# Experts of a fused attention and mixture kernel: columns reordered, conversion spread differently, gates loaded first, a branch hint moved

## The chip, the cores and the metric
The kernel runs on one core of a Trainium2 chip. The metric is the device time of one execution in microseconds; three runs of the kernel before gave a median of 917.99 us (917.13 to 922.21). The kernel after computes the same outputs.

## What is computed
The program has three parts, one behind the other.

```python
# attention, for every batch and head, token by token (B 4, H 8, S 768, D 48)
y[:, :, t] = einsum('bhd,bhde->bhe', q[:, :, t], state)
v_old = einsum('bhde,bhd->bhe', state, k_n[:, :, t])
state = state + beta_t * einsum('bhd,bhe->bhde', k_n[:, :, t], v_t - v_old)
# experts: 3072 tokens of 384 columns, 8 experts of width 1024
expert_idx = argmax((x_n @ e_n.T) / tau)          # one expert per token
out[mask] = gate_w[mask] * (relu(x[mask] @ w1[e]) @ w2[e])
# dense layers of width 2048
h = relu(x @ w_in);  result = (h * h) @ w_out
```

## The kernel before
**Order.** All instructions are put on the five engines in the order of the program text (a manual schedule), and each engine works through its own queue in order. TensorE multiplies; ScalarE and VectorE empty PSUM and convert; GpSimd issues indirect transfers; SP issues the plain transfers, all into one queue.

**Attention** runs in 24 steps of 32 tokens. `PW` (L385 on) ends a step: ScalarE copies the step's 128 x 384 outputs from a PSUM bank to the rows `XG` (L401), with the sign turned. From there the next step's `xrt` transposes them on TensorE for the router's logits (against the normalized expert embedding `enT` made in `router_consts`), `squares` takes the norm, and GpSimd scatters each row into its expert's slots of the DRAM buffer `xs` (L488). Beside the 384 columns a row carries 8 logits, a token number and a norm. The last rows of attention are placed for expert 0 by matmuls (`place`, `turn_x`), without the detour through `xs`; expert 0's first weights are loaded in three pieces during attention (`pre1`, L635 on).

**Splitting.** Every float32 product is done as three matmuls on an upper half and a lower half of each operand (`mm3`, L1172 to L1174). The upper half is written by ScalarE, the lower half by VectorE as the difference. For weights `weights(upto)` does this in pieces of 128 x 768: ScalarE's upper half at L620, and VectorE's lower half at L578 in the next `flush`. Per expert there are four pieces of second weights and four of the next expert's first weights.

**One expert** has capacity for 448 tokens. First half: eight blocks `fb` of 128 hidden columns, each nine matmuls into a PSUM bank (448 or 384 wide, by the count of tokens), then ScalarE's `hh` (L1273) and the 64-wide `ht` (L1274) and VectorE's lower half `hl` (L1275). Blocks 0 to 2 have banks of their own; blocks 3 to 7 and the short tile go round three banks. After each block `run(k)` hands out side work: weights, and steps of the conversion below. Second half: four token tiles in the order 0, 3, 1, 2 (tile 3 is the short one, 64 tokens), each with 24 matmuls (or the `tail` for the short one), an eviction `y` with the gate as scale (L1320), and an indirect scatter of `y` to `x2` by GpSimd (L1323); `run(9)` to `run(12)` follow them. In the second half `run` also pops `x_steps`: three times a VectorE transpose of the next expert's gathered columns `xe` (L1146), ScalarE's upper half (L1149) and VectorE's lower half (L1152). The transpose reads 32 columns at a stride of three elements, because the first weights of experts 1 to 7 lie in SBUF with three consecutive rows to a partition.

**Gates.** In expert 0 the softmax weights of all slots are worked out by the list `gops`, from columns of `xs` fetched by `load_gates` (L939 on; five transfers of 40-byte elements), behind `load_x(1)` in SP's queue.

**Conversion.** `q64` holds 132 steps: 22 pieces (numbers 2 to 23) of the dense layers' weights, six steps each (`w64`, L1084 on; the steps' VectorE lines are L1101, L1105, L1109, L1114, L1120 and L1117). A piece's first step reads its 512 KB load and issues that of the next piece (`fetch64(m + 1)`, L1082); the last writes to `wscr`. How many steps each `run(k)` does stands in the tuples `n`.

**Overflow.** Behind `run(10)` of expert 0, `overflow` holds a long part for experts with more than 448 tokens, under a branch (L989) that all engines evaluate and that skips it here. `mark_branch_hint_location("over", "LikelyTaken")` puts a hint for that branch into the engines' queues. Behind the branch SP loads the next expert's second weights (`load_w2`, four transfers, L1166).

Of the kernel before, what the change touches and what calls it, by code (L numbers as in the profile page):

```python
# [13 lines left out]
AF = mybir.ActivationFunctionType  # L14
ALU = mybir.AluOpType
# [7 lines left out]
def kernel(  # L23
# [16 lines left out]
    nc = tc.nc  # L40
    V, G, A, PE = nc.vector, nc.gpsimd, nc.scalar, nc.tensor
    NT, DM = out.shape
# [342 lines left out]
    def PW(s):  # L385
        g, i = divmod(s, 4)
        for hq in range(2):
            for b in range(4):
                PE.matmul(
                    YP[C * b : C * b + C, hq * 192 : hq * 192 + 192],  # L390
                    PL2[g][:, b, i, hq],
                    Wb[hq][:, b].rearrange("p f e -> p (f e)"),
                    start=s + hq == 0,
                    stop=True,
                    skip_group_check=True,
                )
        if i == 0:
            XG[g] = rp.tile([128, 4, ROW], F32, name="XG", bufs=3)
            G.tensor_copy(XG[g][:, :, XT].bitcast(I32), tok_i[:, 4 * g : 4 * g + 4])
            G.memset(XG[g][:, :, XT + 2 :], 0.0)  # L400
        A.activation(XG[g][:, i, 0:DM], YP[:, :DM], AF.Copy, scale=-1.0)  # L401
        if s >= NS - 2:
            hi, lo = [kept[0][:, (2 * i + j - 4) * DM : (2 * i + j - 3) * DM] for j in range(2)]
            A.activation(hi, XG[g][:, i, 0:DM], AF.Copy)
            lows.append(lambda: V.tensor_tensor(lo, XG[g][:, i, 0:DM], hi.bitcast(F32), ALU.subtract))
            oh = kept[0][:, 4 * DM + (i - 2) * CAP : 4 * DM + (i - 1) * CAP]
            more.append(([hi, lo], oh))
# [136 lines left out]
    def router_consts():  # L544
        nc.scalar.dma_start(itau, moe_tau.rearrange("(a b) -> a b", a=1).broadcast_to([128, 1]))
        emb = rp.tile([E, DM], F32, name="emb")
        nc.scalar.dma_start(emb, moe_expert_emb)
        jk = rp.tile([128, DM], F32, name="junk")[:E]
        es = rp.tile([E, 4], F32, name="es")
        A.activation(jk, emb, AF.Square, accum_out=es[:, 0:1])  # L550
        ops = []
        newton(ops, es[:, 1:2], es[:, 0:1], es[:, 2:3], magic[:E, :1])
        ops.append(lambda: V.reciprocal(itau, itau))
        ops.append(lambda: V.reciprocal(es[:, 1:2], es[:, 1:2]))
        ops.append(lambda: V.tensor_scalar(emb, emb, es[:, 1:2], None, ALU.mult))

        def turn():
            for kc in range(KD):
                PE.transpose(XP[:, kc * E : (kc + 1) * E], emb[:, kc * 128 : (kc + 1) * 128], ident[:E, :E])
            A.activation(enT.rearrange("p a e -> p (a e)"), XP[:, : KD * E], AF.Copy)  # L560

        ops.append(turn)
        return ops
# [71 lines left out]
    def pre1(a, fetch):  # L635

        if wbuf[0] is None:
            wbuf[0] = [None] * 4
        if fetch:
            raw1[a] = wp.tile([128, C, C], F32, name="AL", bufs=3).rearrange("p i j -> p (i j)")  # L640
            nc.sync.dma_start(raw1[a], moe_w1[0, a * 128 : a * 128 + 128])
            return
        wbuf[0][0] = wbuf[0][0] or cp.tile([128, 3072], F32R, name="W", bufs=5)
        V.tensor_copy(part(wbuf[0], 0, a * 1024, 1024), raw1[a])
# [340 lines left out]
    def overflow(mp):  # L985
# [3 lines left out]
        with tc.If(anyo > 0, label="over"):  # L989
# [18 lines left out]
            for e in range(E):  # L1008
                ne = nc.values_load(nover[0:1, e : e + 1], min_val=0, max_val=most)
                with tc.For_i(0, ne, 1) as i:  # L1010
                    b1 = mp.tile([128, 2304], F32, name="hb")
                    b2 = spare[0]
                    w, xg = b1[:, :1536], b1[:, 1536 : 1536 + ROW]
                    h, xt, y = b2[:, :1024], b2[:, 1024 : 1024 + DM], b2[:, 1024 + DM : 1024 + 2 * DM]
                    nc.sync.dma_start(xg, xs[bass.ds(i * 128 + (SLOTS + e * OVR), 128)])
                    ps = PT[0]
                    for kc in range(KD):
                        PE.transpose(ps[:, kc * 128 : kc * 128 + 128], xg[:, kc * 128 : kc * 128 + 128], ident)
                    A.activation(xt, ps[:, :DM], AF.Copy)
                    w1 = moe_w1[e].rearrange("(a p) f -> p a f", p=128)  # L1020
                    w2 = moe_w2[e].rearrange("(a p) f -> p a f", p=128)
                    for c in range(2):
                        nc.sync.dma_start(
                            w.rearrange("p (a f) -> p a f", a=KD), w1[:, :, c * 512 : c * 512 + 512]
                        )
                        ps = PT[1]
                        for fb in range(4):
                            for kc in range(KD):
                                o = kc * 512 + fb * 128
                                PE.matmul(  # L1030
                                    ps[:, fb * 128 : fb * 128 + 128],
                                    w[:, o : o + 128],
                                    xt[:, kc * 128 : kc * 128 + 128],
                                    start=kc == 0,
                                    stop=kc == KD - 1,
                                )
                        A.activation(h[:, c * 512 : c * 512 + 512], ps, AF.Relu)
                    ps = PT[2]
                    for c in range(2):
                        nc.sync.dma_start(w.rearrange("p (a f) -> p a f", a=4), w2[:, c * 4 : c * 4 + 4])  # L1040
                        for fb in range(4):
                            PE.matmul(
                                ps[:, :DM],
                                h[:, (c * 4 + fb) * 128 : (c * 4 + fb) * 128 + 128],
                                w[:, fb * DM : fb * DM + DM],
                                start=c + fb == 0,
                                stop=c + fb == 4,
                            )
                    ga, ops = gate(mp, xg[:, XL : XT + 2].unsqueeze(1), mp.tile([128, 4], F32, name="gsmo"), "gateo")
                    for o in ops:  # L1050
                        o()
                    A.activation(y, ps[:, :DM], AF.Copy, scale=ga)
                    G.indirect_dma_start(
                        out=x2,
                        out_offset=bass.IndirectOffsetOnAxis(ap=xg[:, XT : XT + 1].bitcast(U32), axis=0),
                        in_=y,
                        in_offset=None,
                        bounds_check=NT - 1,
                        oob_is_err=False,
                    )  # L1060
# [61 lines left out]
    def moe():  # L1122
# [14 lines left out]
        def x_steps(e):  # L1137
# [4 lines left out]
            for a in range(KD):  # L1142

                def turn(a=a):
                    x = xt[a] = mp.tile([128, CAP], F32, name="xt")
                    V.transpose(  # L1146
                        x.rearrange("p (u t) -> p u t", t=C), xe[e].rearrange("p u (k a) -> p a u k", a=KD)[:, a]
                    )
                    A.activation(xh[e][:, a], x, AF.Copy)  # L1149

# [64 lines left out]

        w_pieces()
        load_w2(0)
        load_x(1)
        t2k = mp.tile([128, 512], F32, name="t2k", bufs=3)
        gx = t2k[:, :320].rearrange("p (t e c) -> p t e c", t=4, e=E)  # L1220
        load_gates(gx)
        ga, gops = gate(mp, gx.rearrange("p t e c -> p (t e) c"), t2k[:, 320:448])
        ga = ga.rearrange("p (t e) -> p t e", t=4)
        rows_i = mp.tile([128, 4, E], I32, name="rows")
# [4 lines left out]
        for e in range(E):  # L1229
            wt = wbuf[e % 2]  # L1230
            def run(k, e=e):
# [4 lines left out]
                    weights(8 * e + (1, 1, 2, 3, 4, 4, 5, 5, 6, 8, 10, 11)[k - 1])  # L1236
                else:
                    weights(8 * e + (1, 1, 2, 3, 4, 4, 5, 5, 6, 7, 8, 8)[k - 1])
                n = (0, 0, 0, 0, 0, 0, 0, 0, 5, 5, 4, 0) if e == 0 else (0, 2, 0, 0, 0, 2, 0, 2, 4, 4, 3, 0)
                if last:  # L1240
                    n = (0, 2, 1, 0, 0, 2, 0, 2, 5, 4, 0, 0)
                for j in range(n[k - 1]):
                    if q64:
                        q64.popleft()()
# [10 lines left out]
            for fb in range(8):  # L1255
# [15 lines left out]
                        skip_runtime_bounds_check_because="it is only compared",  # L1271
                    )
                A.activation(hh[:, fb], ps[:, :384], AF.Relu)  # L1273
                A.activation(ht[:, fb], ps[:, 384:CAP], AF.Relu)  # L1274
                V.scalar_tensor_tensor(  # L1275
                    hl[:, fb], ps[:, :384], 0.0, hh[:, fb].bitcast(F32), ALU.max, ALU.subtract
                )
                run(fb + 1)
            if e == 0:
                while gops:  # L1280
                    gops.pop(0)()
# [10 lines left out]
            for i, t in enumerate((0, 3, 1, 2)):  # L1292
# [12 lines left out]
                def none(wt=wt, ps=ps, hh=hh):  # L1305
                    PE.matmul(ps[:, :64], hh[:, 7, :128], part(wt, 0, 3072, 64), start=True, stop=True)

                if t < 3:
                    for fb in range(8):
                        o = 3072 + fb * DM  # L1310
# [2 lines left out]
                            part(wt, 0, o, DM), part(wt, 1, o, DM), fb == 0, fb == 7,  # L1313
                        )
                else:
                    if e == 0:
                        tc.mark_branch_hint_location("over", "LikelyTaken", engines=ENGINES)
                    by_count(e, tail, none)
                y = mp.tile([128, DM], F32, name="y", bufs=2)
                A.activation(y[128 - n :], ps[128 - n :, :DM], AF.Copy, scale=ga[128 - n :, t, e : e + 1])  # L1320
# [151 lines left out]
```

## Time and profile before

| | us |
|---|---|
| median of 3 runs (lowest, highest) | 917.99 (917.13, 922.21) |
| the profiled execution | 918.82 |
| its span, first to last instruction | 917.0 |
| TensorE busy with matmuls | 851.9 |
| VectorE busy | 605.8 |
| ScalarE busy | 443.2 |
| GpSimd busy | 102.8 |

Attention takes the span up to about 268 us, the experts up to about 507, the dense layers the rest. Rows of a timeline give start and length in us, engine, line and operation; in brackets how long the engine was idle before, and what ended that. A row of the windows view gives a stretch and its length, then busy time and count of PE, PEld (the loads of weights), DVE, ACT and POOL, the granted clock, the share of the transfer engines and GB/s. ScalarE is named ACT, VectorE DVE, TensorE PE, GpSimd POOL, SP's queue SPq; a q behind an engine's name is its sequencer. Tile names are the program's: `wb` and `W` are weights' halves, `t4k` the conversion's input, `lb` a buffer whose parts hold second weights, `ht` and a conversion's intermediate.

### The profile page before, as it was taken

To read this page: it belongs to the slowest core of one execution; us is meant where nothing else is said; L and a number is where in the kernel's file an instruction comes from. 1 tells how busy PE (TensorE), PEld (TensorE's weight loads), DVE (VectorE), ACT (ScalarE), POOL (GpSimd) and SP (SyncE) were. 2 spreads that over 40 slices of the span, in tenths; PEclk is the share of its full clock that TensorE was granted. 3 is DMA by queue.
4 is the path that set the end of the run, shared out by engine and by line. 5 is a ranking of instruction groups with operands and counts; after the bars stand their busy time and mean duration, and the time that the engine had idled before them with its cause. 6 is when DMAs were issued, how large, how long until landed. Compare 5 with 4: busy or idle time off the path is not lost.

```text
span 917.0 us, 21827 instructions
## 1 busy us (share of the span) xinstructions
PE 851.9 (93%) x8775; PEld 777.3 (85%) x8775; DVE 605.8 (66%) x1499; ACT 443.2 (48%) x1074; POOL 102.8 (11%) x138
## 2 busy tenths in 40 slices
PE   4668989989987999999999999999999999999998
PEld 2446767667775989899888899999999999999998
DVE  6999899999777799889888762607061533425150
ACT  2246777778843565556555652515051423324140
POOL 3012103212210222122222100000000000000000
PEclk7587899999999999999999999999999999999999
DMA  8795775441139697788764632010010102020000
GB/s 331 243 281 178 227 222 145 166 153 62 67 115 198 217 299 217 216 251 237 236 216 159 182 87 44 1 39 15 18 35 18 35 9 44 9 44 1 26 1 27
DMA packets 110735, 116.27 MB, mean 127 GB/s; under 512 B 72771, under 2 KB 89258, under 8 KB 110624
## 3 DMA queue, kind: packets, MB, share of 16 engines
q1 hardware_dynamic: 102400, 88.39, 33.7%
q0 software_dynamic: 8064, 26.35, 7.8%
q8 instruction: 75, 1.23, 0.6%
q14 instruction: 36, 0.29, 0.1%
q10 hardware_dynamic: 160, 0.01, 0.0%
HBM read 82.61 MB, written 32.89 MB: 126 GB/s over the span
## 4 chain that ended last, share of the span: by engine, by line
PE 54%; DVE 5%; DMA 3%; issue 2%; ACT 2%; another core or an unknown queue 0%; POOL 0%; SPq 0%; DVEq 0%; POOLq 0%; ACTq 0%
PE gp L1172 7%; PE gp L1174 7%; PE gp L1173 7%; PE xp L1172 4%; PE xp L1174 4%; PE xp L1173 4%; PE sp L1173 3%; PE sp L1172 3%; PE sp L1174 3%; PE yp L1172 3%; PE yp L1174 3%; PE yp L1173 3%; DMA t4k<-in_moe_w_out_dram 1%; PE gp L1300 1%; DMA lb<-in_moe_w_dram 1%
## 5 line engine op out<-in xcount | busy, mean ns | idle before, releaser
L1380 DVE TENSOR_TENSOR t4k<-t2k 128x384 f32<-128x384 f32 x128 | 71.4, 558 | 199.7 <-ACT t2k L1379 197.7
L272 DVE TENSOR_TENSOR TL<-TL,tmp 128x135 f32<-128x135 f32 (+15 forms) x186 | 60.9, 338 | 1.8
L264 DVE TENSOR_TENSOR tmp<-AL,TL 128x135 f32<-128x135 f32 (+15 forms) x186 | 60.6, 337 | 1.6
L1172 PE MATMUL xp<-wb,hh 128*128 128x384 f32 x184 | 61.5, 334 | 0.0
L1173 PE MATMUL xp<-wb,hh 128*128 128x384 f32 x184 | 61.5, 334 | 0.0
L1174 PE MATMUL xp<-wb,hl 128*128 128x384 f32 x184 | 61.5, 334 | 0.0
L1323 POOL DMA_INDIRECT x<-y,rows x32 | 37.6, 1176 | 155.7 <-ACT y L1320 69.3
L1172 PE MATMUL sp<-xh,W 128*128 128x384 f32 (+1 forms) x156 | 52.6, 337 | 1.4 <-ACT xh L979 1.1
L1173 PE MATMUL sp<-xl,W 128*128 128x384 f32 (+1 forms) x156 | 52.5, 336 | 0.6 <-DVE xl L980 0.6
L1174 PE MATMUL sp<-xh,W 128*128 128x384 f32 (+1 forms) x156 | 52.4, 336 | 0.0
L1172 PE MATMUL gp<-wb,hh 128*128 128x384 f32 x152 | 51.2, 337 | 0.0
L1174 PE MATMUL gp<-wb,hl 128*128 128x384 f32 x152 | 50.8, 334 | 0.0
L1173 PE MATMUL gp<-wb,hh 128*128 128x384 f32 x152 | 50.8, 334 | 0.0
L367 ACT ACTIVATE Sb<-sp 48x384 f32<-48x384 f32 x92 | 44.7, 486 | 11.5 <-PE sp L357 10.5
L1173 PE MATMUL yp<-xl,W 128*128 128x384 f32 (+1 forms) x147 | 49.3, 335 | 0.0
L1172 PE MATMUL yp<-xh,W 128*128 128x384 f32 (+1 forms) x147 | 49.3, 335 | 0.0
L1174 PE MATMUL yp<-xh,W 128*128 128x384 f32 (+1 forms) x147 | 49.3, 335 | 0.0
L1404 ACT ACTIVATE y<-gp 128x384 f32<-128x384 f32 x12 | 5.9, 492 | 81.9 <-PE gp L1174 81.9
L1174 PE MATMUL gp<-xh,W 128*128 128x384 f32 (+1 forms) x135 | 45.2, 335 | 0.0
L1172 PE MATMUL gp<-xh,W 128*128 128x384 f32 (+1 forms) x135 | 45.2, 335 | 0.0
L1173 PE MATMUL gp<-xl,W 128*128 128x384 f32 (+1 forms) x135 | 45.2, 335 | 0.0
L1404 ACT ACTIVATE y<-xp 128x384 f32<-128x384 f32 x12 | 5.9, 492 | 80.2 <-PE xp L1174 80.2
(355 smaller groups left out, 2478.3 us busy)
## 6 DMA issues: line engine op xcount, KB each, us to landing
W<-in_moe_w_dram SPq DMA_DIRECT2D x28, 384.0 KB
hb<-in_moe_w_dram SPq DMA_DIRECT2D x24, 384.0 KB
W<-wscr SPq DMA_DIRECT2D x16, 384.0 KB
W<-in_kq_dram SPq DMA_DIRECT2D x11, 512.0 KB
wscr<-t2k POOLq DMA_DIRECT2D x22, 256.0 KB, 6.4
xs<-padrow POOLq DMA_DIRECT2D x8, 693.0 KB, 7.7
t4k<-in_moe_w_in_dram SPq DMA_DIRECT2D x10, 512.0 KB
xe<-xs SPq DMA_DIRECT2D x28, 168.0 KB
```

The lines of the kernel that those rows point to most:

```text
L264: V.tensor_tensor(tv[0], AL[:, j, j + 1 :].unsqueeze(1).broadcast_to([128, n, m]), T[:, :n, j : j + 1].broadcast_to([128, n, m]), ALU.mult,)
L272: V.tensor_tensor(T[:, : j + 1, j + 1 :], T[:, : j + 1, j + 1 :], tv[0], ALU.add)
L367: A.activation(Sb[hq][r : r + D, :, :, par, :], SP_[hq][r : r + D, 0:384].rearrange("p (b m e) -> p b m e", b=4, m=2), AF.Copy,)
L1172: PE.matmul(ps, hs, rh, start=first, stop=False)
L1173: PE.matmul(ps, hs, rl, start=False, stop=False)
L1174: PE.matmul(ps, ls, rh, start=False, stop=last)
L1300: PE.matmul(ps[64 * r : 64 * r + 64, :DM], ht[:, 4 * r + fb], w2raw[e][4 * r + fb], start=fb == 0, stop=fb == 3,)
L1323: to_x2 = lambda n=n, t=t, y=y, e=e: G.indirect_dma_start(out=x2, out_offset=bass.IndirectOffsetOnAxis(ap=rows_i[:n, t, e : e + 1].bitcast ...
L1380: V.tensor_tensor(s2, r, r, ALU.mult)
L1404: A.activation(y, ps[:, :DM], AF.Copy)
```

## The change
The rows' columns are written in the order in which the transposes of the experts read them, so that these read contiguous columns; the embedding, expert 0's first weights and the overflow part follow that order. The gates' columns are loaded ahead of expert 1's tokens. The conversion's 132 steps are spread 19, 6 x 16, 17 instead of 14, 6 x 17, 16. The 64-wide eviction goes behind `run`. The hint goes in front of expert 0's first token tile.

```diff
@@ PW
-        A.activation(XG[g][:, i, 0:DM], YP[:, :DM], AF.Copy, scale=-1.0)
+        A.activation(
+            XG[g][:, i, 0:DM].rearrange("p (q a k) -> p q k a", q=4, a=KD),
+            YP[:, :DM].rearrange("p (q k a) -> p q k a", q=4, a=KD),
+            AF.Copy,
+            scale=-1.0,
+        )
@@ router_consts (the transposes below it read jk instead of emb)
-        ops.append(lambda: V.tensor_scalar(emb, emb, es[:, 1:2], None, ALU.mult))
+        ops.append(
+            lambda: V.tensor_scalar(
+                jk.rearrange("e (q a k) -> e q k a", q=4, a=KD),
+                emb.rearrange("e (q k a) -> e q k a", q=4, a=KD),
+                es[:, 1:2], None, ALU.mult,
+            )
+        )
@@ pre1
-            nc.sync.dma_start(raw1[a], moe_w1[0, a * 128 : a * 128 + 128])
+            for m in range(4):
+                q, i = divmod(4 * a + m, KD)
+                rows = moe_w1[0, 96 * q : 96 * q + 96].rearrange("(k a) f -> a k f", a=KD)[i]
+                nc.sync.dma_start(raw1[a][32 * m : 32 * m + 32], rows)
...
@@ x_steps
-                        x.rearrange("p (u t) -> p u t", t=C), xe[e].rearrange("p u (k a) -> p a u k", a=KD)[:, a]
+                        x.rearrange("p (u t) -> p u t", t=C), xe[e].rearrange("p u (a k) -> p a u k", a=KD)[:, a]
@@ moe
         load_w2(0)
-        load_x(1)
         t2k = mp.tile([128, 512], F32, name="t2k", bufs=3)
         gx = t2k[:, :320].rearrange("p (t e c) -> p t e c", t=4, e=E)
         load_gates(gx)
+        load_x(1)
@@ run
-                n = (0, 0, 0, 0, 0, 0, 0, 0, 5, 5, 4, 0) if e == 0 else (0, 2, 0, 0, 0, 2, 0, 2, 4, 4, 3, 0)
+                n = (0, 0, 0, 0, 0, 0, 0, 0, 6, 5, 5, 3) if e == 0 else (0, 2, 0, 0, 0, 2, 0, 2, 4, 3, 3, 0)
                 if last:
-                    n = (0, 2, 1, 0, 0, 2, 0, 2, 5, 4, 0, 0)
+                    n = (0, 2, 1, 0, 0, 2, 0, 2, 5, 4, 1, 0)
@@ the first half's blocks
                 A.activation(hh[:, fb], ps[:, :384], AF.Relu)
-                A.activation(ht[:, fb], ps[:, 384:CAP], AF.Relu)
                 V.scalar_tensor_tensor(
                     hl[:, fb], ps[:, :384], 0.0, hh[:, fb].bitcast(F32), ALU.max, ALU.subtract
                 )
                 run(fb + 1)
+                A.activation(ht[:, fb], ps[:, 384:CAP], AF.Relu)
@@ the second half's tiles
+                if e == 0 and i == 0:
+                    tc.mark_branch_hint_location("over", "LikelyTaken", engines=ENGINES)
                 if t < 3:
...
                 else:
-                    if e == 0:
-                        tc.mark_branch_hint_location("over", "LikelyTaken", engines=ENGINES)
                     by_count(e, tail, none)
```

## Rows read from the trace of the kernel before

**Rows 1.** Windows view, a stretch of experts 0 and 1; busy us (and count) by engine.

```profile
320.00:340.00 20.00, 18.30 (x103) 17.41 (x102) 19.04 (x31) 11.25 (x24) 5.15 (x6) 1.00 1.01 298
```

**Rows 2.** Waits of PE, 290 to 600 us: total us, times, longest.

```profile
PE xp L1172 <- PEq L989: 5.2, 1, 5.2
PE ch L1174 <- DVE wb L578: 2.5, 2, 1.4
PE ch L1174 <- DVE W L578: 2.4, 2, 1.5
PE gp L1174 <- DVE hl L1275: 1.4, 1, 1.4
```

**Rows 3.** Windows view behind the branch, columns as in rows 1.

```profile
298.00:301.00 3.00, 2.85 (x9) 2.88 (x10) 1.72 (x3) 2.34 (x4) 0.29 (x1) 0.50 0.03 5
```

**Rows 4.** Timeline of PE, expert 1's last blocks, expert 2's first.

```profile
317.38 0.41 PE L1172 MATMUL sp<-xh,wb 128*128 128x384 f32 x1
...
319.05 0.33 PE L1172 MATMUL yp<-xh,wb 128*128 128x384 f32 x1
...
336.97 0.44 PE L1174 MATMUL ch<-xh,W 128*128 128x384 f32 x1 [1.49 <-DVE W L578]
```

**Rows 5.** Timeline of DVE in expert 0.

```profile
285.94 0.19 DVE L1225 COPY rows<-t2k 128x32 int32<-128x32 int32 x1 [3.60 <-DMA t2k<-xs]
...
292.39 0.36 DVE L1101 TENSOR_SCALAR W<-t4k 128x512 int32<-128x512 int32 x1
...
299.82 0.61 DVE L1322 SCALAR_TENSOR_TENSOR y<-gp,gate,y 64x384 f32<-64x384 f32 x1 [1.25 <-ACT y L1320]
...
302.20 0.69 DVE L1117 SCALAR_TENSOR_TENSOR t2k<-lb,t2k 128x512 f32<-128x512 f32 x1
```

**Rows 6.** Chain that ended last, in order of time: start, us, what.

```profile
310.82 8.23 DMA lb<-in_moe_w_dram
...
352.67 0.28 ACT y L1320
...
363.85 0.47 PE ch L1174
```

**Rows 7.** Groups by line and form, DVE transposes: count, busy us, mean ns.

```profile
L1146 DVE STREAM_TRANSPOSE xt<-xe 128x448 f32<-128x448 f32 x21 | 16.3, 775 | 0.0
L277 DVE STREAM_TRANSPOSE TTt<-TL 128x256 f32<-128x256 f32 x24 | 15.7, 672 | 0.0
...
L1201 DVE STREAM_TRANSPOSE y<-xe 128x384 f32<-128x384 f32 x21 | 12.0, 573 | 0.0
```

**Rows 8.** Timeline of ACT in an attention step, the eviction L401 and the work behind.

```profile
190.77 0.49 ACT L401 ACTIVATE XG<-yp 128x384 f32<-128x384 f32 x1
191.88 1.36 ACT L329 ACTIVATE Ub<-ch 32x192 f32<-32x192 f32 x4 [0.61 <-PE ch L308]
```

**Rows 9.** Timeline of SP's queue: x of expert 1, gates, expert 1's second weights.

```profile
272.58 2.80 SPq L1133 DMA_DIRECT2D xe<-xs  x4
275.43 7.09 SPq L943 DMA_DIRECT2D t2k<-xs  x3
282.56 1.34 SPq L945 DMA_DIRECT2D t2k<-xs  x2
...
309.36 1.42 SPq L1166 DMA_DIRECT2D hb<-in_moe_w_dram  x3
```

**Rows 10.** Timeline of DVE in expert 1's first half.

```profile
306.73 0.96 DVE L578 TENSOR_TENSOR wb<-W,wb 128x768 fp32r<-128x768 f32 x1 [1.05 <-DVEq L989]
...
323.58 0.55 DVE L1275 SCALAR_TENSOR_TENSOR hl<-yp,hh 128x384 fp32r<-128x384 f32 x1
...
324.91 0.42 DVE L1101 TENSOR_SCALAR W<-t4k 128x512 int32<-128x512 int32 x1
```

**Rows 11.** Timeline of POOL, the short tile's scatter in expert 0.

```profile
300.71 1.52 POOL L1323 DMA_INDIRECT x<-y,rows  x1 [5.85 <-DVE y L1322]
```

**Rows 12.** Timeline of DVE at the end of the last expert.

```profile
503.69 0.69 DVE L1117 SCALAR_TENSOR_TENSOR t2k<-lb,t2k 128x512 f32<-128x512 f32 x1
```

More of the change, by code (lines that the diff above doesn't have):

```diff
@@ L554, in router_consts @@
         ops.append(lambda: V.reciprocal(es[:, 1:2], es[:, 1:2]))
-        ops.append(lambda: V.tensor_scalar(emb, emb, es[:, 1:2], None, ALU.mult))
+        ops.append(
[5 more added lines that the diff above has]
+        )
         def turn():
             for kc in range(KD):
-                PE.transpose(XP[:, kc * E : (kc + 1) * E], emb[:, kc * 128 : (kc + 1) * 128], ident[:E, :E])
+                PE.transpose(XP[:, kc * E : (kc + 1) * E], jk[:, kc * 128 : (kc + 1) * 128], ident[:E, :E])
             A.activation(enT.rearrange("p a e -> p (a e)"), XP[:, : KD * E], AF.Copy)
@@ L1016, in overflow @@
                     ps = PT[0]
+                    A.activation(
+                        y.rearrange("p (q k a) -> p q k a", q=4, a=KD),
+                        xg[:, 0:DM].rearrange("p (q a k) -> p q k a", q=4, a=KD),
+                        AF.Copy,
+                    )
                     for kc in range(KD):
-                        PE.transpose(ps[:, kc * 128 : kc * 128 + 128], xg[:, kc * 128 : kc * 128 + 128], ident)
+                        PE.transpose(ps[:, kc * 128 : kc * 128 + 128], y[:, kc * 128 : kc * 128 + 128], ident)
                     A.activation(xt, ps[:, :DM], AF.Copy)
```

## The prediction, made before the change was run

> **What bounds the kernel now.** The windows view came first: in the experts' stage TensorE and VectorE are both close to full [rows 1], while the dense layers behind it keep TensorE busy throughout. So only idle time of TensorE between 268 and 515 us can be gained. The waits of TensorE name it [rows 2]: 5.2 us for its own sequencer at the branch around the overflow part (L989), 4.9 us in four waits for VectorE's lower halves of the next expert's first weights (L578), and 1.4 us for a lower half of the hidden tile. [...]
>
> The timelines and the chain then show who sets the pace. In expert 0 VectorE waits 3.60 us for the gates' columns and does gate arithmetic until 292.39 [rows 5]. The chain of waits runs through the load of expert 1's second weights [rows 6], not through TensorE's branch: what TensorE loses there, VectorE and the transfers lose as well.
>
> **The change part by part.** *Columns in VectorE's order.* 21 transposes of 128x448 read every third element in 0.775 us; 128x384 in order take 0.573 [rows 7], so 448 in order should take 0.573 x 448/384 = 0.67 at most, and less if part of it is fixed cost. I take 0.655: 0.12 saved each, 0.36 per expert. In return 24 evictions on ScalarE scatter their 384 elements 128 bytes apart. No row has such a write on ScalarE. Nearest is the 128x256 transpose that strides on both sides, 0.672 [rows 7], against 0.573 x 256/384 = 0.38 in order: 0.29 us for 256 elements, so between 0 and 0.43 for 384 if all of it is the write's. ScalarE idles 0.61 us behind this eviction in a step [rows 8], which covers that; after the last steps it is bare. I take 0.1 once, bounds 0 and 0.6. [...] The nine extra loads of weights lie steps ahead of their use, behind nothing that waits on SP; the reordered embedding is 8 rows, once. Both nothing; should the loads come late, the cast at L644 would wait for them.
>
> *Gates first.* Today x's four issues take SP 2.80 us from 272.58, then the gates' five 7.09 + 1.34, ending at 283.90 [rows 9]; they land 2.0 us later, at 285.94 [rows 5]. Issued first they end at 281.0 and land at 283.1. VectorE is free for them at 285.94 - 3.60 = 282.3. I take 282.7: all that follows on it is 3.2 us earlier, and TensorE's waits for the hidden tile go. x lands some 3 us later, still ahead of its first transpose.
>
> *The hint* moves from in front of the short tile to in front of the first tile, 24 matmuls (4 us) earlier on TensorE. [...]
>
> *Spread 19.* In expert 0's second half VectorE does the sixth step of a piece (0.69) and one more subtraction of about that size in the 1.25 us that it idles before 299.82 [rows 5]; with three faster transposes the short tile's y comes at 299.82 - 3.2 - 0.36 = 296.3. GpSimd scatters it [rows 11], and SP loads expert 1's second weights 309.36 - 300.71 = 8.65 us after that scatter's start [rows 9, 11], because the skipped branch waits for its landing: now at 305.8. VectorE goes on from 296.9: two lower halves (1.8), five steps (0.42 to 0.69, 0.58 in the mean: 2.9), the branch (1.05 [rows 10]), a lower half 0.9: 303.5. TensorE's first block of expert 1 ends there, some 6 us earlier than today.
> Then come five steps, a lower half, and steps 17 to 19, at about 308.6. Steps are six to a piece, so step 19 begins piece 5, and reads a 512 KB load that SP issues behind the four loads of expert 1's second weights. Today VectorE comes to it at 324.91 [rows 10] and sees no wait. The last of the four lands 8.23 us after its issue at 310.82 [rows 6], 9.7 after the first; the piece behind it lands 9.7 to 11.0 after (512 KB at 400 GB/s take 1.3). I take 10.2, so 316.0: **a new wait of 7.4 us on VectorE.** Queued behind it are the hidden tile's halves of expert 1, and with them PSUM banks. TensorE has banks for six blocks, done at 303.5 + 5 x 1.6 = 311.5; the seventh waits for the fourth half. VectorE gets there through the step 0.4, two halves 1.0, a weights' half 0.87, two steps 1.15 and two halves 1.0: 320.4, where the block begins at 317.38 now [rows 4]. TensorE is 3.0 late, and after some 9 us idle I expect the low clock again, 1.5 for about nine matmuls as after the 5.2 us [rows 3].
> On VectorE the eighth half, which ends at 324.1 now [rows 10], ends 10.1 after the wait, at 326.1. By VectorE, expert 2's first block resumes 336.97 - 324.1 = 12.9 later [rows 4, 10] less 0.9 (one step, three transposes): 338.1. By TensorE its first output tile comes 4.5 late, about 329.3; from there to the resumption expert 2 shows 363.85 - 352.67 = 11.2 [rows 6], less 0.8: 339.7. I take 339.4 against 336.97: **+2.4**, bounds +1.1 and +2.8.
>
> *16 each.* At the boundaries into experts 3, 5 and 6 VectorE has one step less (0.42 to 0.69) and two faster transposes ahead of the late half: 0.8 each, 2.4 in all, less what ScalarE's own order of evictions keeps. I take **-1.7**, bounds -2.4 and -0.5.
>
> *17 in the last expert.* One step is pushed behind the others, in front of the iota on GpSimd that the final gather waits for; VectorE's last step, 0.69, ends at 504.4 now [rows 12]. **+0.6**, bounds 0 and +0.7.
>
> *64-wide evictions later.* 0.1 us less before each upper half, and a bank that is freed behind a split. TensorE waits for VectorE there, so nothing; where a split waits for its load, the bank waits with it, at most 0.8 once.
>
> Sum: 2.4 - 1.7 + 0.6 + 0.1 = +1.4. The profiled execution took 918.82 (its span 917.0 and 1.8 around it), 0.83 above the median of 917.99. Profiled: 920.2; median: **919.4**.
>
> **The rivals.** *The load is no wait* (faster). If piece 5 lands by 308.6, expert 1 keeps its lead: -3.6 by the earlier weights' load and -0.9 by VectorE's lighter half, so -4.5 - 1.7 + 0.6 + 0.1 = -5.5: 912.5. Against it: it stands behind 1.5 MB in one queue. For it: the whole queue moves forward, and each microsecond of earlier landing is one gained.
> *The weights' load does not move* (slower). If it stays at 309.36, since the skipped branch waits for some other transfer, piece 5 lands at 319.6 and the seventh block comes 3.6 later than in my sum: +5.0, 923.0. It decides from a landing at about 319.2 on. Against it: the row before the load is GpSimd's scatter, which VectorE's y leads.
> *The scattered write.* If an eviction grows by more than the 0.61, each step pays the rest: 0.2 over would be 23 x 0.2 = 4.6, and 924.0 in all. The bound of 0.43 speaks against.
> *The hint does nothing.* TensorE then stands 5.2 us at the branch and comes to expert 1 near 304, still ahead of the wait on step 19: 919.4 too. [...]
>
> **How the numbers follow.** Forecast 0.55 (the hint working 0.35 or not 0.20), no wait 0.25, load unmoved 0.14, scattered write 0.06. A measurement of this kernel can tell about 0.5% (4.6 us) from no change: faster 0.25, same 0.55, slower 0.20. The range reaches from 911.5, below the first rival, to 924.0, over the second; outside lie about 0.10 of the first, and 0.10 of the second and third. The likeliest case alone: 917 to 922.
>
> **What would show it.** Right: the gates' first instruction on VectorE near 282.7; expert 1's first block near 299 to 304; a wait of several microseconds on VectorE before the conversion's first step (L1101) near 309 to 316, and TensorE's longest wait of the stage behind it; transposes near 0.65; about 0.6 less wait at each of three later boundaries. Wrong: no such wait (then faster), an eviction of the columns above 1.1 us, or the weights' load still at 309.

## The result, and the profile after

| | before | after |
|---|---|---|
| median of 8 runs, us | 920.34 | 929.39 |
| ratio, 95% interval | | 1.0090 (1.0063 to 1.0118) |
| profiled execution, its span, us | 918.82, 917.0 | 931.17, 929.4 |
| start of the experts' stage on TensorE | 267.83 | 270.55 |
| length of the experts' stage | 245.08 | 253.27 |
| from there to the end | 404.1 | 405.6 |

The kernel became slower by 0.9%, some 8 us. The stage is counted from the last matmul of the count of tokens (`xp<-cum,ones`) to the first product of the dense layers. Its length is given beside the ratios because attention's end varied from 267.6 to 274.1 us between the profiles below, with either order of the columns. Each length comes from one profiled execution; how much it varies between executions of one kernel was not measured. Of the 12.4 us between the two spans 2.7 lie in attention, 8.2 in the experts, 1.5 in the dense layers.

TensorE's waits of the kernel after, 290 to 620 us (line; total us, times, longest), against [rows 2]:

```profile
PE sp L1191 <- ACT lb L1297: 9.3, 2, 8.2
PE ch L1193 <- DVE wb L589: 3.9, 3, 2.2
PE ch L1193 <- DVE W L589: 1.7, 2, 1.0
PE sp L1191 <- ACT xh L993: 1.6, 1, 1.6
PE xp L1191 <- PEq L1003: 1.0, 1, 1.0
```

The stall at the branch fell from 5.2 to 1.0 and the wait for the hidden tile's half is gone. In their place stands one wait of 8.2 us, and it is for ScalarE's 64-wide eviction `ht` (L1297, tile name `lb`), not for VectorE. The timelines of expert 1 show how it comes about; first VectorE, SP's queue and TensorE:

```profile
311.24 0.69 DVE L1136 SCALAR_TENSOR_TENSOR t2k<-lb,t2k 128x512 f32<-128x512 f32 x1
318.88 0.43 DVE L1120 TENSOR_SCALAR W<-t4k 128x512 int32<-128x512 int32 x1 [6.94 <-DMA t4k<-in_moe_w_in_dram]
319.22 0.55 DVE L1293 SCALAR_TENSOR_TENSOR hl<-ch,hh 128x384 fp32r<-128x384 f32 x1
320.44 0.56 DVE L1293 SCALAR_TENSOR_TENSOR hl<-ch,hh 128x384 fp32r<-128x384 f32 x1 [0.67 <-ACT hh L1292]
...
324.06 0.56 DVE L1293 SCALAR_TENSOR_TENSOR hl<-sp,hh 128x384 fp32r<-128x384 f32 x1 [0.67 <-ACT hh L1292]
```

```profile
307.57 1.42 SPq L1185 DMA_DIRECT2D hb<-in_moe_w_dram  x3
309.03 0.50 SPq L1185 DMA_DIRECT2D lb<-in_moe_w_dram  x1
309.57 1.43 SPq L1101 DMA_DIRECT2D t4k<-in_moe_w_in_dram  x2
```

```profile
324.93 0.69 PE L1191 MATMUL sp<-xh,wb 128*128 128x384 f32 x1 [8.18 <-ACT lb L1297]
```

Step 19's first instruction waits 6.94 us for the load that SP issued behind the four of expert 1's second weights. It lands 318.88 - 307.57 = 11.3 us after the first of them. ScalarE in the same stretch:

```profile
308.49 0.46 ACT L1292 ACTIVATE hh<-ch 128x384 fp32r<-128x384 f32 x1
310.98 0.85 ACT L631 ACTIVATE wb<-hb 128x768 fp32r<-128x768 f32 x1 [2.03 <-DMA hb<-in_moe_w_dram]
319.81 0.22 ACT L1297 ACTIVATE lb<-ch 128x64 f32<-128x64 f32 x1 [7.98 <-DVE hl L1293]
319.93 0.48 ACT L1292 ACTIVATE hh<-ch 128x384 fp32r<-128x384 f32 x1
...
324.66 0.23 ACT L1297 ACTIVATE lb<-sp 128x64 f32<-128x64 f32 x1
```

ScalarE's 64-wide eviction of block 0 stood 7.98 us, until VectorE had its lower half of the same block, and with it every upper half behind it in ScalarE's queue. Both only read the bank, but one comes behind the other. Before, VectorE's half came behind ScalarE's two evictions; the waits of VectorE before, and of ScalarE after (285 or 290 to 520 us):

```profile
DVE hl L1275 <- ACT lb L1274: 13.2, 16, 2.6
```

```profile
ACT lb L1297 <- DVE hl L1293: 30.2, 32, 8.0
```

In the list of ScalarE's waits before no such line stands. So one read depends on the other: `ACT lb` waits for `DVE hl` 32 times after, 30.2 us in all, and never before. The direction turned with the order of the program's text, as these two lists show. Why the two reads of one bank are kept apart no run here shows.

### The profile page after: what moved, and what is told of

Read it like the earlier page. It is cut to its first block, busy times and chain, and to the rows that moved or that the text cites. A ratio compares the mean times of both kernels' runs of the same rounds, so it can differ in the third digit from the quotient of the medians.

```text
span 929.4 us, 21763 instructions
## 1 busy us (share of the span) xinstructions
PE 859.9 (93%) x8775; PEld 783.0 (84%) x8775; DVE 605.0 (65%) x1499; ACT 455.2 (49%) x1074; POOL 99.5 (11%) x138
## 4 chain that ended last, share of the span: by engine, by line
PE 54%; DVE 5%; issue 3%; DMA 3%; ACT 2%; POOL 0%; SPq 0%; POOLq 0%; ACTq 0%; DVEq 0%
PE gp L1191 7%; PE gp L1193 7%; PE gp L1192 7%; PE xp L1191 4%; PE xp L1193 4%; PE xp L1192 4%; PE sp L1191 3%; PE sp L1192 3%; PE sp L1193 3%; PE yp L1191 3%; PE yp L1193 3%; PE yp L1192 3%; DMA x<-y,rows 1%; DVE W L589 1%; DMA t4k<-in_moe_w_in_dram 1%
## 5 line engine op out<-in xcount | busy, mean ns | idle before, releaser
L357 PE MATMUL sp<-Wb,kL 128*48 128x96 f32 x736 | 46.3, 276 | 2.3 <-issue 1.7
L1191 PE MATMUL gp<-xh,W 128*128 128x384 f32 (+1 forms) x135 | 45.2, 335 | 0.0
```

Of the source, the lines that this page charges most:

```text
L357: PE.matmul(SP_[hq][64 * par : 64 * par + D, b * 96 : b * 96 + 96], kL2[g][:, i, b * 2 + hq], Wb[hq].rearrange("p b (m r) e -> p b r m e", ...
L1191: PE.matmul(ps, hs, rh, start=first, stop=False)
```

## The experiments

In each table row below "vs before" is the ratio with its interval, and in us the change that this ratio makes of the median of before measured beside it; "stage" is the length of the experts' stage in the profile (before 245.1, after 253.3).

**One part back.** Into the changed kernel: `u_ht` the 64-wide eviction in its old place, `u_spread` the old tuples of `n`, `u_ht_spread` both, `u_cols` the columns in the old order in all places.

```diff
@@ u_ht
                 A.activation(hh[:, fb], ps[:, :384], AF.Relu)
+                A.activation(ht[:, fb], ps[:, 384:CAP], AF.Relu)
...
                 run(fb + 1)
-                A.activation(ht[:, fb], ps[:, 384:CAP], AF.Relu)
@@ u_spread
-                n = (0, 0, 0, 0, 0, 0, 0, 0, 6, 5, 5, 3) if e == 0 else (0, 2, 0, 0, 0, 2, 0, 2, 4, 3, 3, 0)
+                n = (0, 0, 0, 0, 0, 0, 0, 0, 5, 5, 4, 0) if e == 0 else (0, 2, 0, 0, 0, 2, 0, 2, 4, 4, 3, 0)
...
-                    n = (0, 2, 1, 0, 0, 2, 0, 2, 5, 4, 1, 0)
+                    n = (0, 2, 1, 0, 0, 2, 0, 2, 5, 4, 0, 0)
```

`u_ht`:

> The changed kernel with its 64-wide eviction back in front of VectorE's half. Theory A (the eviction behind the split ties ScalarE to VectorE, as both read one PSUM bank and are kept apart there, so after the 6.9 us wait the upper halves come one by one): the seventh block of expert 1 begins about 4.4 us after that wait's end instead of 6.05, and the whole is 1.6 to 3.5 us faster than the changed kernel, +5.5 to +7.5 us against the kernel before. Rival B (only the wait on step 19's load counts): within 0.5 us of the changed kernel, +9. Rival C (attention's scattered write made the 9 us): +9 too.

`u_spread`:

> The changed kernel with the conversion spread as before (14, 6 x 17, 16). Theory A and B (step 19 waits for the 512 KB load behind expert 1's second weights): the 6.9 us wait on VectorE is gone and the 8.2 us wait of TensorE with it; 5 to 9 us faster than the changed kernel, 0 to +4 us against the kernel before. Rival C (attention): +7 or more remain, and TensorE's first block of expert 0 still starts some 2.7 us later than before.

`u_ht_spread`:

> Both of the two parts back. Theory A: the eviction also costs at the later boundaries, so -4 to +1 us against the kernel before, 1 to 3 us less than with the spread alone back. Rival B: the same as with the spread alone back, within 0.7 us. Rival C: +3 or more remain.

`u_cols`:

> The changed kernel with the columns in the old order in all places. Theory A and B: the write's extra 0.41 us per step is hidden in attention and the faster transposes give back about 0.1 us each where VectorE is late: between 1 us faster and 2 us slower than the changed kernel, +8 to +11 us against the kernel before. Rival C (the scattered write costs attention 2.7 us or more): 2.5 to 9 us faster than the changed kernel, 0 to +6.5.

| | vs before | us | stage |
|---|---|---|---|
| u_ht | 1.0016 (0.9991 to 1.0041) | +1.5 | 248.2 |
| u_spread | 0.9985 (0.9955 to 1.0014) | -1.4 | 246.3 |
| u_ht_spread | 0.9949 (0.9914 to 0.9983) | -4.7 | 241.5 |
| u_cols | 1.0109 (1.0076 to 1.0141) | +10.1 | 253.3 |

Attention (C) falls: with the columns back the loss stays, and with either of the other two back most of it goes. The spread's return brought some 10 us by the ratios, a little more than A said, and 7.0 us of the stage. B falls as well: the eviction alone is worth 0.74% of the 0.9% by the ratios, more than the 1.6 to 3.5 us that A gave it, and 5.1 us of the stage. Both back give -4.7, just under A's range, and a stage 4.8 us shorter than the spread alone back, where A had 1 to 3. `u_cols` lies in its range, and its stage is as long as that of after: beside the other parts the faster transposes gained nothing there.

The mechanism shows in VectorE's and TensorE's timelines of `u_ht`:

```profile
317.56 0.43 DVE L1120 TENSOR_SCALAR W<-t4k 128x512 int32<-128x512 int32 x1 [5.75 <-DMA t4k<-in_moe_w_in_dram]
317.91 1.01 DVE L1294 SCALAR_TENSOR_TENSOR hl<-ch,hh 128x384 fp32r<-128x384 f32 x2
...
320.76 1.01 DVE L1294 SCALAR_TENSOR_TENSOR hl<-sp,hh 128x384 fp32r<-128x384 f32 x2
```

```profile
321.93 0.66 PE L1191 MATMUL sp<-xh,wb 128*128 128x384 f32 x1 [3.58 <-DVE hl L1294]
```

ScalarE has worked ahead, so lower halves follow each other in pairs ("x2") without the 0.67 us gaps of the kernel after, and the seventh block starts 321.93 - 317.56 = 4.37 us behind the wait's end, where it was 324.93 - 318.88 = 6.05. The rest of the eviction's price lies later: counted from the stage's start, after stands 1.1 us behind `u_ht` where expert 2 begins, 1.8 at expert 4, 3.2 at expert 6, 5.3 at expert 7. In expert 6 the low clock adds to it (windows view from that expert's first block on, of after, then of `u_ht`; columns as in [rows 1]):

```profile
452.90:462.90 10.00, 8.82 (x34) 7.10 (x33) 8.01 (x14) 5.66 (x12) 2.79 (x4) 0.83 0.68 236
```

```profile
449.00:459.00 10.00, 9.07 (x44) 7.94 (x44) 6.99 (x12) 6.17 (x15) 3.17 (x3) 1.00 0.60 199
```

The first ten microseconds hold 34 matmuls at a granted clock of 0.83 and 44 at 1.00. Whether that clock is owed to the eviction is open (last section).

**Direction or place; the load; the hint.** `u_ht_mid` takes the eviction from behind the split, but leaves it behind VectorE's half in the text: ScalarE's order is that of `u_ht`. `u_load` issues step 19's load ahead of expert 1's second weights; `u_ht_load` is that with the eviction in its old place; `u_hint` has the hint in its old place.

```diff
@@ u_ht_mid
-                run(fb + 1)
                 A.activation(ht[:, fb], ps[:, 384:CAP], AF.Relu)
+                run(fb + 1)
@@ u_load, u_ht_load
-        if m < len(pieces64):
+        if m < len(pieces64) and m not in raw64:
...
                 if e == 0 and i == 1:
+                    fetch64(5)
                     overflow(mp)
```

`u_ht_mid`:

> The changed kernel with the 64-wide eviction ahead of the split again, but still behind VectorE's half in the program: ScalarE's order is the old one, and only who waits for whom differs (ScalarE's 64-wide read for VectorE's read of the same bank). Theory A (the tie to VectorE costs): most of the loss stays, +6.5 to +10 us against the kernel before, and in expert 1 ScalarE's 64-wide evictions still stand idle until VectorE's halves. Rival D (it is the place behind a split, whose load is late, that costs): like the kernel with the eviction fully back, +0 to +3.

`u_load`:

> The changed kernel with step 19's 512 KB load issued at the end of the second token tile of expert 0, ahead of expert 1's second weights in SP's queue. Theory A (that load's place in the queue makes the wait): VectorE's 6.9 us wait shrinks below 1 us, TensorE's 8.2 us wait to some 2 us, and the whole to between -3 and +2 us against the kernel before (the spread alone back gave -1.4). Rival E (the transfer engines are full then, wherever the load stands): a wait of 3 us or more stays and the whole is above +4.

`u_ht_load`:

> The same early load, and the 64-wide eviction back in front. Theory A: both losses gone with all gains kept, so below the kernel with spread and eviction back (-4.7): -8 to -4 us against the kernel before. Rival E: above -2.

`u_hint`:

> The changed kernel with the hint back in front of the short tile. Theory A (the hint starts the fetch, but expert 1 waits for its weights' halves anyway): TensorE stands some 5 us at the branch again, and the whole is within 2 us of the changed kernel, +7 to +11. Rival F (the stall shrank for another reason, such as the eviction's order): the stall stays near 1 us.

| | vs before | us | stage |
|---|---|---|---|
| u_ht_mid | 1.0214 (1.0179 to 1.0250) | +19.7 | 266.7 |
| u_load | 1.0006 (0.9981 to 1.0031) | +0.6 | 246.9 |
| u_ht_load | 0.9959 (0.9932 to 0.9985) | -3.8 | 242.0 |
| u_hint | 1.0080 (1.0052 to 1.0107) | +7.4 | 253.1 |

`u_ht_mid` settles the eviction, and beyond what A expected: with the same order on ScalarE, the direction of the dependency alone is worth 18.6 us of the stage (266.7 against 248.2). ScalarE's wait for VectorE doubles against after; in its queue the weights' splits now stand behind the eviction too:

```profile
ACT lb L1296 <- DVE hl L1293: 61.1, 59, 8.2
```

Behind the split, where the change put it, the eviction costs less than it does directly behind VectorE's half (stage 253.3 against 266.7). D falls.

In `u_load` VectorE comes to step 19 without a wait, as A expected:

```profile
312.15 0.69 DVE L1136 SCALAR_TENSOR_TENSOR t2k<-lb,t2k 128x512 f32<-128x512 f32 x1
312.75 0.42 DVE L1120 TENSOR_SCALAR W<-t4k 128x512 int32<-128x512 int32 x1
```

TensorE's wait for the eviction shrinks from 8.2 to 2.5 us. VectorE still waits 3.6 us for a load of the conversion in `u_load`, but in expert 0, in front of the first step. So step 19's wait was the place in the queue, and E falls. `u_ht_load`, at -3.8, misses the range of -8 to -4 by a little: without the wait the new spread is worth no more than the old one (stage 242.0 against 241.5).

`u_hint` has the stall of 4.9 us back and the changed kernel's time. The hint's new place is not all that decides: in nine profiles with it the stall was 1.0 to 1.8 in four and 4.5 to 5.4 in five, `u_ht` (5.2) among them, `u_ht_load` with the same place of the eviction among the short ones (1.5). So it is not the eviction's order (F). What it is stays open; that the hint starts a fetch, as A had it, was the author's guess, which no run shows. Between `u_hint` and the changed kernel the stall made no difference to the time.

**One part alone**, in the kernel before: `b_ht` the eviction, `b_spread` the tuples, `b_cols` the columns, `b_hint_gates` the gates' load and the hint. The diffs are the parts of the change itself.

`b_ht`:

> The kernel before with the 64-wide eviction moved behind VectorE's half and the split, and nothing else. Theory A (the tie of ScalarE to VectorE costs by itself): +3 to +6 us against the kernel before, most of it in experts 0 and 1. Rival G (it costs only beside the wait of step 19, which makes the tie felt): within 1.5 us of the kernel before.

`b_spread`:

> The kernel before with the conversion spread 19, 6 x 16, 17 and nothing else. Theory A (step 19's load lands behind expert 1's second weights, whatever stands ahead): a wait of 3 to 7 us on VectorE before that step's first instruction, +3 to +8 us. Rival H (without the gates' earlier load VectorE comes later than the load lands): no such wait, -2 to +1.

`b_cols`:

> The kernel before with the columns in the new order and nothing else. By the prediction's terms: transposes 0.65, the write 0.41 us longer but hidden: -2 to +1 us. Rival C (the write costs attention): +3 or more.

`b_hint_gates`:

> The kernel before with the gates' columns loaded first and the hint moved, and nothing else. By the prediction's terms: the gates' first instruction on VectorE some 3 us earlier after expert 0's start, TensorE's waits for the hidden tile gone, expert 1's second weights earlier by 2 to 4 us: -1 to -4 us. Rival (VectorE's gain is lost in its next wait): within 1 us.

| | vs before | us | stage |
|---|---|---|---|
| b_ht | 1.0048 (1.0013 to 1.0083) | +4.4 | 249.8 |
| b_spread | 1.0041 (1.0012 to 1.0071) | +3.8 | 251.5 |
| b_cols | 0.9950 (0.9922 to 0.9979) | -4.6 | 242.8 |
| b_hint_gates | 0.9976 (0.9951 to 1.0002) | -2.2 | 245.0 |

A holds for the eviction and the spread, G and H fall. Where the eviction costs was missed: only 1.8 of its 4.7 us lie ahead of expert 2, where A had most of it. `b_spread` shows the wait with the gates loaded late:

```profile
313.93 0.69 DVE L1117 SCALAR_TENSOR_TENSOR t2k<-lb,t2k 128x512 f32<-128x512 f32 x1
320.92 0.43 DVE L1101 TENSOR_SCALAR W<-t4k 128x512 int32<-128x512 int32 x1 [6.29 <-DMA t4k<-in_moe_w_in_dram]
```

In `b_hint_gates` the gates start 3.8 us earlier and expert 1's second weights are loaded 2.5 us earlier, as expected, but where expert 3 begins nothing of it is left (92.96 us after the stage's start, before 93.03). The stage is as long as before, and the ratio's interval reaches over 1, so the rival (the gain is lost in the next wait) is not excluded.

By stage lengths the parts add up: +4.7 +6.4 -2.3 -0.1 = +8.7, where the change as a whole has +8.2. The ratios' sum, +1.4, does not reach the whole's +8.3. The gap of 6.9 us is near what the five intervals (2.4 to 3.2 us to either side) leave together, 6.0 as the root of the sum of their squares, so whether the parts interact stays open. The columns alone gained more than expected. The fastest mixtures tried are `u_ht_spread`, columns, gates and hint without the spread and the eviction, and `b_cols`, the columns alone: both are below both kernels, and the ratios do not tell them apart.

## Why the prediction was wrong

Forecast 919.4 with a range to 924.0, measured 929.39. Of these 10.0 us, 2.35 lie in the base: the median of before was 917.99 in the three runs behind the forecast and 920.34 in the eight of the result. Moved by that, the range would end at 926.4, still below. Times on the trace below are counted from the stage's start, to take out attention's 2.7 us.

**The step that failed** is the last of the parts: "64-wide evictions later ... TensorE waits for VectorE there, so nothing; where a split waits for its load, the bank waits with it, at most 0.8 once." It asked only when the bank comes free. Who has to wait for whom to read it was not asked, although the edit turned that round: an engine that ran ahead was put behind the slower one, once per block, for 64 blocks of the stage, and at half of them it waited. Measured: 5.1 us of the stage in the changed kernel and 4.7 alone; between `u_spread` and `u_ht_spread` it is 4.8 and between `u_load` and `u_ht_load` 4.9, so four pairs of profiles agree.

**The term that was too small** is that of the spread with the lead ahead of it, +2.4. Much of its course came as forecast: the gates' first instruction 18.11 → 14.36 (predicted -3.2, measured -3.75), the second weights' load 41.53 → 37.02 (-3.6, -4.5), the wait from 41.4 to 48.3, 6.9 long (predicted 40.8 to 48.2, 7.4), and with the eviction back the seventh block 49.55 → 52.11, +2.6 (+3.0). Some of this is luck. GpSimd's scatter was only 3.0 earlier, but the weights' load followed it by 7.1 us instead of 8.65, which the sum had taken as fixed (that it waits for this scatter's landing was the author's reading; in before SP's wait of 2.4 us ahead of that load ended with a DMA); and the conversion's load came 11.3 after the first of the four, beyond the 9.7 to 11.0 of the sum, whose 400 GB/s are near the 412 that the transfers moved from 315 to 321 us in before (windows view).

Expert 2 then resumed 3.5 later in `u_ht` (69.14 → 72.67) and 4.6 in the kernel after (73.74), above the upper bound of 2.8. By the terms of the rival "the load is no wait" the +2.4 is a lead of 4.5 and a wait that costs 6.9. `u_ht_load`, the same parts without the wait, resumes expert 2 at 66.46: a lead of 2.7, and a wait that costs 6.2. So the wait was priced about right, and the lead was too large. One place where it goes was not in the sum: with the gates early, VectorE comes to the conversion's first step ahead of its load (kernel after).

```profile
292.67 0.43 DVE L1120 TENSOR_SCALAR W<-t4k 128x512 int32<-128x512 int32 x1 [1.24 <-DMA t4k<-in_moe_w_in_dram]
```

The low clock behind the long wait was expected for nine matmuls, for 1.5 us, which is half of the 3.00 us at a granted clock of 0.50 in [rows 3]. It lasted twice as long in `u_ht`, through the seventh and eighth block (first two rows), and for one block in the kernel after (third row):

```profile
321.90:324.90 3.00, 2.98 (x9) 3.00 (x10) 3.00 (x5) 0.57 (x3) 0.00 (x0) 0.50 0.01 4
324.90:327.70 2.80, 2.80 (x11) 2.80 (x11) 2.17 (x4) 1.34 (x3) 0.00 (x0) 0.55 0.31 64
```

```profile
324.90:328.00 3.10, 3.07 (x10) 3.07 (x11) 3.10 (x5) 1.92 (x5) 0.00 (x0) 0.53 0.00 0
```

The two blocks took 5.7 us in `u_ht` and 4.6 in the kernel after, where before had 3.2: 2.5 and 1.3 lost, though TensorE had stood 3.6 us in the former and 8.2 in the latter. The low level, 0.50 to 0.55, is near the 0.50 of [rows 3].

**What held.** *Transposes*: predicted 0.655, measured 0.637 (groups by line and form, count, busy us, mean ns). The later boundaries gave less than forecast, but within their bounds: from expert 2's resumption to the stage's end `u_ht` needs 175.5 where before had 175.9, -0.4 against the -1.1 of "16 each" and "17" together.

```profile
L1165 DVE STREAM_TRANSPOSE xt<-xe 128x448 f32<-128x448 f32 x21 | 13.4, 637 | 0.0
```

21 x 0.138 = 2.9 is also about what the columns alone gave back in the stage (2.3), more than the sum had let them count for; in the changed kernel, by the stage of `u_cols`, they gave back nothing. *The scattered write*: 0.49 → 0.90 (the row has shortest, median and longest in ns), just under the upper bound of +0.43; why the scattered write takes longer no run here shows:

```profile
L401 ACT ACTIVATE XG<-yp x24: 826/901/930, 63.3 to 258.5; 128x384 f32<-128x384 f32 x24
```

The idle time behind it covered it: from 183 us on attention's steps take 7.1 to 8.1 us with the old write and 7.2 to 7.9 with the new one, but for the last. *The hint*: no effect on the time, as predicted (`u_hint` +7.4 us, the changed kernel +8.3). With its new place the stall was 4.5 to 5.4 us in five profiles and 1.0 to 1.8 in four. A short stall (1.0 us in the kernel after) did not keep the slow clock away: after its 2.2 us wait in expert 1's first block the kernel after ran eleven matmuls at 0.59 (306.8 to 310.0 us). *The other rivals*: "the load is no wait" and "the weights' load does not move" fell by the same rows that bore out the wait.

The change without its failed step is `u_ht`: +1.5 us (-0.8 to +3.8) where the sum was +1.4. The interval holds the sum, but that the two are so near is luck: the stage of `u_ht` is 3.1 longer than before, from the +3.5 and the -0.4 above. With the failed step set right the sum would have been 1.4 + 5.1 = +6.5, within the interval of the change's own ratio (+5.8 to +10.9 us).

## What to carry to other kernels

When an instruction that reads a PSUM bank is moved past another engine's reader of the same bank, ask which of the two now waits, and what is queued behind the one that waits: here a short eviction put behind the slower engine's tied the faster engine to it, block after block (32 waits, 30.2 us). Ask whether a step that starts a new transfer stands ahead of a bulk load in the queue or behind it: here VectorE waited 6.94 us for the load issued behind, and not at all for it in `u_load`, where it was issued ahead. Count steps against the point where a new piece begins. Undo parts one at a time: here the gain that one part has alone was hidden under the losses of two others.

## What was not expected of the hardware

The granted clock differed between profiles with the same waits. In the first block of expert 6 TensorE stands 1.00 us for a lower half in the kernel after and in `u_load` alike; over the ten microseconds from that expert's first product on the clock was 0.83 in the former (the row above) and 1.00 in the latter (windows view of `u_load`):

```profile
447.20:457.20 10.00, 8.80 (x41) 7.26 (x40) 8.03 (x14) 6.02 (x12) 2.69 (x4) 1.00 0.69 237
```

What decides between them, and whether it is the kernel or the single execution, no run here tells.

At the start of the dense layers the profiles fall into two groups in the same way, 404.0 to 404.1 or 405.3 to 405.7 us from there to the end; before and after are in different ones (windows view of after, then of before):

```profile
523.80:527.00 3.20, 2.54 (x10) 2.28 (x11) 1.97 (x4) 0.73 (x2) 0.99 (x1) 0.81 0.57 188
```

```profile
512.90:516.00 3.10, 2.45 (x12) 2.19 (x13) 1.97 (x4) 1.00 (x3) 0.00 (x0) 1.00 0.84 293
```

That is 1.5 us of the difference between the two profiled spans that belongs to no edit in particular: `u_ht_spread`, without both losses, is in the slower group too, and `u_ht_load`, with all the parts but the eviction and with the early load, in the faster one.
